# A routed two-layer network behind decayed attention: the weight narrowing's transfers move from SyncE's queue to ScalarE's

## The chip, the cores and the metric

The kernel runs on one core of a Trainium2 chip. A core has five engines that each work through their own list of instructions in order: TensorE (PE, matrix products; PEld is its loading of weights), VectorE (DVE), ScalarE (ACT), GpSimd (POOL) and SyncE (SP). They wait for each other through semaphores. SP computes nothing here; it reads a number and issues DMA transfers, which 16 DMA engines carry out. [...] The metric is the device time of one execution in microseconds (us), the median of three runs.

## What is computed

Three stages, in 32-bit floats. The 64-bit `w_in` and `w_out` at the end are the input's; the kernel gets them as raw 64-bit words (see below).

```python
# 1. causal attention without softmax, decayed by gamma_h ** (i - j): batch 4, 8 heads, 576 rows, 64 columns
scores = (q @ k.T) / sqrt(64)
x = (scores * Dmat) @ v                        # -> 2304 tokens of 512 features
# 2. each token goes to one of 8 experts, 288 tokens each, by descending logit x @ w_gate
order = np.argsort(-(x @ w_gate).flatten())    # first come, first served, until an expert is full
h = np.maximum(x[mask] @ w1[e], 0.0)           # 288 x 512 @ 512 x 1024
out[mask] = h @ w2[e]                          # 288 x 1024 @ 1024 x 512
# 3. a gated network over all tokens
h = x @ w_in                                   # 2304 x 512 @ 512 x 2048
out = (h * tanh(softplus(h))) @ w_out          # 2304 x 2048 @ 2048 x 512
```

## The kernel before

**Stages.** The attention fills the first 100 us. Behind it runs the expert stage: for each of eight experts, in the order in which they fill up, a search on VectorE and PE (the routing) finds the expert and its 288 tokens, GpSimd gathers the tokens' rows (`xg`), PE transposes them (`mmx`), and PE does 96 first products (`mma`, eight groups of 12) and 96 second products (`mmb`, four outputs of 24). Last come the products of the gated network, in six tiles of 384 tokens (`mmc` and `po`).

**Three products for one.** Products run in a reduced 32-bit format. Each operand is therefore split in a rounded part and a rest, and each product is done three times. For an expert's weights that is the work of `unit` and `split_unit`: SP loads a tile of 512 KB (`st`, five buffers), ScalarE rounds it (`whi`, L564), and GpSimd or VectorE subtracts (`wlo`, L567), which frees the `st` buffer. Eight such units make an expert. ScalarE and VectorE split the activations likewise: `xh` and `xl` of the gathered tokens, `hh` and `hl` of the first products' results. ScalarE also copies each second product from its bank to a buffer `y` (four of them, `YB`), which SP stores.

**The expert's number.** VectorE makes it (`eid`, L532). SP reads it (`value_load`, L534), for the address of the eight loads that follow.

**The list store.** SP stores the token numbers of an expert (`list_scratch`, L652): 288 numbers of 4 bytes, as 96 rows of 3.

**The narrowing.** [...] `narrow()` makes 32-bit copies of `w_in` and `w_out` from their 64-bit words, in 32 pieces beside the experts' work. For a piece SP loads 512 KB (`std`, three buffers); ScalarE scales the high words (`words`, one buffer in PSUM); VectorE shifts these and joins them with the low words' top bits (`words`, then `dw`, L730 and L733); ScalarE takes the sign (`dt`, L737); GpSimd multiplies (`dw`, L741); SP stores 256 KB (L744). The last stage's units are loaded from these copies.

**What sets the order.** A planner (`run_tasks`) writes every engine's list before the program runs. Each piece of work is a generator that yields an engine, an estimated duration, what must come before, and a priority; the planner takes, at estimated times, the first ready piece and appends its instructions to that engine's list. An estimate doesn't hold anything up on the chip, but the order that comes of it does: an instruction that waits there holds all that stands behind it on its engine.

Of the kernel before, what the change touches and what calls it, by code (L numbers as in the profile page):

```python
# [7 lines left out]
F32 = mybir.dt.float32  # L8
# [3 lines left out]
U32 = mybir.dt.uint32  # L12
# [5 lines left out]
P = 128  # L18
# [16 lines left out]
APART = 3000  # L35
NRING = 12
STAGES = 5
YB = 4
CLOSED = -1.0e37

PE, DVE, POOL, ACT, SP = "pe", "dve", "pool", "act", "sp"
HOP = 200
DMA_RATE = 350
DMA_ISSUE = 100
# [88 lines left out]
class Kernel:  # L133
# [389 lines left out]
    def weights_of(self, junk, at, i):  # L523

        nc, a, rw = self.nc, self.a, self.rw
        units = {}
        self.weights.append(units)
        n0 = len(self.weights) * 8 - 8
        at = yield DVE, 160, [at], EID
        eid = rw.tile([P, 1], I32, name="eid")  # L530
        with nc.allow_low_precision(reason="small integers"):
            nc.vector.tensor_reduce(eid, junk, AX.X, ALU.add)  # L532
        at = yield SP, 1000, [at if i == 0 else Event(at.t + APART)], 0
        e = nc.sync.value_load(eid[0:1, 0:1], min_val=0, max_val=E - 1)  # L534
        for u in range(8):
            if u < 4:
                src = a["w1"][bass.ds(e, 1), :, u * 256:(u + 1) * 256]
            else:
                src = a["w2"][bass.ds(e, 1), (u - 4) * 256:(u - 3) * 256, :]
            yield from self.unit(n0 + u, src.rearrange("o (k p) c -> p (o k) c", p=P),  # L540
                                 DVE if n0 == 0 and u < 2 else None, units, 3,
                                 *([lambda: self.fetched] if n0 == 0 and u == FIRST_UNITS else []))
# [122 lines left out]
    def y_place(self):  # L665

        n = self.made - YB
        return Event(0) if n < 0 else self.stored[n] if n < len(self.stored) else None
# [38 lines left out]
    def narrow(self):  # L707

        nc, v, ic, a = self.nc, self.nc.vector, self.ic, self.a
        done = {k: {} for k in ("load", "read", "turn", "shift", "sign", "store")}  # L710

        def at(k, n):
            return [lambda: done[k].get(n)] if n >= 0 else []

        def load():
            for n in range(32):
                name = ("w_in", "w_out")[n % 2]
                c, r = divmod(n // 2, a[name].shape[0] // P)
                r = slice(r * P, r * P + P)
                now = yield SP, DMA_ISSUE, [Event(0), *[lambda: self.apart(e()) for e in at("read", n - 3)]], self.narrow_priority  # L720
                st = self.conv.tile([P, 512, 2], U32, name="std", bufs=3)
                nc.sync.dma_start(st.rearrange("p c w -> p (c w)"), a[name].bitcast(U32)[r, c * 1024:c * 1024 + 1024])
                self.spawn(piece(n, st, self.arrival(524288, now), a[name + "32"][r, c * 512:c * 512 + 512]))

        def piece(n, st, now, dst):
            high, w = st[:, :, 1].bitcast(F32), self.words.bitcast(U32)
            now = yield ACT, 680, [now, *at("read", n - 1)], self.narrow_priority
            nc.scalar.activation(self.words, high, AF.Copy, scale=2.0 ** -112)
            now = yield DVE, 620, [now], self.narrow_priority
            v.tensor_scalar(w, w, ic[:, IC["three"]], None, op0=ALU.logical_shift_left)  # L730
            now = yield DVE, 680, [now, *at("store", n - 2)], self.narrow_priority
            out = self.conv.tile([P, 512], U32, name="dw", bufs=2)
            v.scalar_tensor_tensor(out, st[:, :, 0], ic[:, IC["low"]], w, op0=ALU.logical_shift_right, op1=ALU.bitwise_or)  # L733
            done["shift"][n] = now
            sign = yield ACT, 680, [*at("sign", n - 2), *at("shift", n)], self.narrow_priority
            t = self.conv.tile([P, 512], F32, name="dt", bufs=2)
            nc.scalar.sign(t, high)  # L737
            done["read"][n] = sign
            now = yield POOL, 1310, [now, sign], self.narrow_priority
            out = out.bitcast(F32)  # L740
            nc.gpsimd.tensor_tensor(out, out, t, op=ALU.mult)  # L741
            done["sign"][n] = now
            now = yield SP, DMA_ISSUE, [Event(now.t + APART)], self.narrow_priority
            nc.sync.dma_start(dst, out)  # L744
            done["store"][n] = self.arrival(262144, now)
            self.narrowed[n] = done["store"][n]

        self.spawn(load())

    def product(self, name, terms, first=True, last=True, bank=None):  # L750
# [20 lines left out]
    def experts(self):  # L771
        nc, a = self.nc, self.a
        for i in range(E):
# [14 lines left out]
            def result(i, d, bank, at):  # L788
                at = yield ACT, 410, [at, self.y_place], 0
                self.made += 1  # L790
                y = self.fa.tile([P, CAP], F32, name="y", bufs=YB)
                nc.scalar.copy(y, bank[1][:, :CAP])
# [292 lines left out]
```

## Time and profile before

| | us |
|---|---|
| runs (three) | 886.77, 889.37, 892.02 |
| median | 889.37 |
| the profiled execution's own time | 888.98 |
| its span, first to last instruction | 887.2 |
| PE busy | 805.0 (91%) |
| VectorE, ScalarE, GpSimd busy | 677.7, 408.2, 479.0 |

The profile is of one execution. In its rows a line such as L564 is a line of the kernel; `SPq` is SP issuing a transfer; `x96` counts instructions; a bracket `[7.29 <-ACT y L792]` says that the engine was idle for 7.29 us just before, and which instruction ended the wait. `out<-in` names tiles without their buffer numbers. PEclk is TensorE's granted clock as a share of full speed. A DMA share can read above 1, since it sums the time of packets.

### The profile page before, as it was taken

Reading aid. Unit: us, or ns where it says so; the run is one execution under the profiler, and the core shown is the slowest. Engines: PE = TensorE matmul, PEld = TensorE weight load, DVE = VectorE, ACT = ScalarE, POOL = GpSimd, SP = SyncE. Lnnn points to the kernel's source line nnn. Section 1 sums busy time; section 2 is a strip of 40 time slices with the busy share of each in tenths; the row PEclk is TensorE's granted clock in tenths of the full one; section 3 lists DMA queues with packets and bytes.
Section 4 is the critical chain, followed back from the end, with each engine's and each line's share of the span. In section 5 each row is a group of like instructions: output and inputs, shape, how many; then the busy total and the mean of one; then the engine's idle time right before and its main releaser. Section 6 shows DMA issues by size and latency. Waiting matters only on the chain. (4 is left out here: it accounts for less than half of the span.)

```text
span 887.2 us, 15492 instructions
## 1 busy us (share of the span) xinstructions
PE 805.0 (91%) x5834; PEld 722.4 (81%) x5837; DVE 677.7 (76%) x1102; ACT 408.2 (46%) x736; POOL 479.0 (54%) x408
## 2 busy tenths in 40 slices
PE   7999875959898987784989999999999999999997
PEld 5888734948798887784989998998999999999995
DVE  4444584846586766694776999999899899899894
ACT  1221223524353434454675654655655555555552
POOL 4533026473667656573511866756755755755644
PEclk9999768979798989796998999999999999999999
DMA  9982157786777876699894000100200100100000
GB/s 342 362 265 88 60 184 148 245 133 192 174 239 171 181 252 158 224 227 236 300 338 160 18 1 1 63 10 1 63 9 1 63 10 1 63 10 1 36 1 36
DMA packets 66331, 112.37 MB, mean 127 GB/s; under 512 B 10192, under 2 KB 38224, under 8 KB 66256
## 3 DMA queue, kind: packets, MB, share of 16 engines
q1 hardware_dynamic: 63280, 101.94, 39.8%
q0 software_dynamic: 2976, 9.44, 3.5%
q8 instruction: 46, 0.75, 0.4%
q14 instruction: 29, 0.24, 0.1%
HBM read 88.81 MB, written 22.55 MB: 126 GB/s over the span
## 5 line engine op out<-in xcount | busy, mean ns | idle before, releaser
L994 DVE RECIPROCAL q<-q 128x384 f32<-128x384 f32 x96 | 244.3, 2545 | 11.5 <-ACT q L992 7.2
L567 POOL TENSOR_TENSOR wlo<-st,whi 128x1024 fp32r<-128x1024 f32 x55 | 132.3, 2422 | 74.3 <-ACT whi L564 74.3
L996 POOL TENSOR_TENSOR n<-n,q 128x384 f32<-128x384 f32 x96 | 99.1, 1032 | 112.9 <-DVE q L994 101.8
L964 PE MATMUL mmc<-yl,whi 128*128 128x384 f32 x384 | 130.3, 339 | 5.8 <-DVE yl L924 3.4
L1006 POOL TENSOR_TENSOR gl<-n,gh 128x384 fp32r<-128x384 f32 x96 | 106.6, 1110 | 48.2 <-ACT gh L1004 47.8
L964 PE MATMUL mmc<-yh,whi 128*128 128x384 f32 x384 | 129.7, 338 | 0.7 <-ACT yh L921 0.7
L964 PE MATMUL mmc<-yh,wlo 128*128 128x384 f32 x384 | 130.0, 339 | 0.0
L564 ACT CAST whi<-st 128x1024 fp32r<-128x1024 f32 x80 | 82.6, 1045 | 90.8 <-DMA st<-w 85.3
L1025 PE MATMUL po<-whi,gl 128*128 128x512 f32 x288 | 113.9, 395 | 0.0
L1025 PE MATMUL po<-wlo,gh 128*128 128x512 f32 x288 | 113.7, 395 | 0.0
L1025 PE MATMUL po<-whi,gh 128*128 128x512 f32 x288 | 111.9, 389 | 0.0
L989 DVE SCALAR_TENSOR_TENSOR n<-s 128x384 f32<-128x384 f32 x96 | 103.9, 1084 | 2.6 <-ACT s L982 2.1
L982 ACT ACTIVATE s<-mmc 128x384 f32<-128x384 f32 x96 | 47.1, 491 | 126.3 <-PE mmc L964 121.1
L758 PE MATMUL mma<-xh,whi 128*128 128x288 f32 x256 | 81.4, 318 | 10.4 <-ACT xh L626 10.1
L758 PE MATMUL mmb<-hh,whi 128*128 128x288 f32 x256 | 82.4, 322 | 0.0
L964 PEld LDWEIGHTS mmc<-yl,whi 128*128 128x128 f32 x384 | 72.4, 189 | 11.8 <-DVE yl L924 4.4
L758 PE MATMUL mmb<-hl,whi 128*128 128x288 f32 x256 | 81.1, 317 | 0.0
L758 PE MATMUL mmb<-hh,wlo 128*128 128x288 f32 x256 | 80.9, 316 | 0.0
L758 PE MATMUL mma<-xh,wlo 128*128 128x288 f32 x256 | 80.1, 313 | 0.0
L758 PE MATMUL mma<-xl,whi 128*128 128x288 f32 x256 | 78.7, 307 | 0.1
L964 PEld LDWEIGHTS mmc<-yh,whi 128*128 128x128 f32 x384 | 72.4, 189 | 4.9 <-ACT yh L921 0.9
L741 POOL TENSOR_TENSOR dw<-dw,dt 128x512 f32<-128x512 f32 x32 | 43.0, 1346 | 61.4 <-ACT dt L737 24.9
(149 smaller groups left out, 1636.3 us busy)
## 6 DMA issues: line engine op xcount, KB each, us to landing
st<-w SPq DMA_DIRECT2D x64, 512.0 KB
qk<-qk SPq DMA_DIRECT2D x18, 512.0 KB
kv<-kv SPq DMA_DIRECT2D x18, 512.0 KB
std<-w_in SPq DMA_DIRECT2D x16, 512.0 KB
std<-w_out SPq DMA_DIRECT2D x16, 512.0 KB
x_scratch<-xs SPq DMA_DIRECT2D x18, 256.0 KB
y_scratch<-y SPq DMA_DIRECT2D x32, 144.0 KB
yt<-y_scratch SPq DMA_DIRECT2D x22, 192.0 KB
```

The lines of the kernel that those rows point to most:

```text
L564: self.nc.scalar.copy(dst[0], st)
L567: (self.nc.vector if lo.engine == DVE else self.nc.gpsimd).tensor_tensor(dst[1], st, dst[0].bitcast(F32), op=ALU.subtract)
L741: nc.gpsimd.tensor_tensor(out, out, t, op=ALU.mult)
L758: self.nc.tensor.matmul(bank[1][:, :CAP], al if h == 2 else ah, bl if h == 1 else bh, start=(first and j == h == 0), stop=(last and j == n ...
L964: self.nc.tensor.matmul(bank[1][:, :TILE], (wl if h == 2 else wh)[:, c, cs], x[c][h == 1], start=(c == h == 0), stop=(c == HP - 1 and h == 2))
L982: nc.scalar.activation(s, p, AF.Sigmoid)
L989: v.scalar_tensor_tensor(u, s, 2.0, s, op0=ALU.subtract, op1=ALU.mult)
L994: v.reciprocal(q, q)
L996: nc.gpsimd.tensor_tensor(u, u, q, op=ALU.mult)
L1006: nc.gpsimd.tensor_tensor(gl, u, gh.bitcast(F32), op=ALU.subtract)
L1025: nc.tensor.matmul(po[j], (gl if h == 2 else gh)[:, js], (wl if h == 1 else wh)[:, f % 2], start=(f == h == 0), stop=(f == DFF // P - 1 an ...
```

## The change

The narrowing's loads and stores are issued by ScalarE, in its own queue: right behind the sign of piece n it issues the store of piece n-2 and the load of piece n+3. The first three loads and the last two stores stay with SP. A third `dw` buffer is added, and one of the four `y` buffers is given up for it. In the planner, SP's read of an expert's number now follows the last load of the expert ahead; before, it followed the number by an estimated 3 us.

```diff
--- before.py
+++ after.py
@@ -35,7 +35,7 @@
 APART = 3000
 NRING = 12
 STAGES = 5
-YB = 4
+YB = 3
 CLOSED = -1.0e37
 
 PE, DVE, POOL, ACT, SP = "pe", "dve", "pool", "act", "sp"
@@ -530,7 +530,7 @@
         eid = rw.tile([P, 1], I32, name="eid")
         with nc.allow_low_precision(reason="small integers"):
             nc.vector.tensor_reduce(eid, junk, AX.X, ALU.add)
-        at = yield SP, 1000, [at if i == 0 else Event(at.t + APART)], 0
+        at = yield SP, 1000, [at, *([lambda: self.loaded.get(n0 - 1)] if n0 else [])], 0
         e = nc.sync.value_load(eid[0:1, 0:1], min_val=0, max_val=E - 1)
         for u in range(8):
             if u < 4:
@@ -712,38 +712,59 @@
         def at(k, n):
             return [lambda: done[k].get(n)] if n >= 0 else []
 
+        name = ("w_in", "w_out")
+        words, sent = {}, {}
+
+        def place(n):
+            c, r = divmod(n // 2, a[name[n % 2]].shape[0] // P)
+            return name[n % 2], slice(r * P, r * P + P), c
+
+        def fetch(n, queue):
+            if n < 32:
+                w, r, c = place(n)
+                words[n] = self.conv.tile([P, 512, 2], U32, name="std", bufs=3)
+                queue.dma_start(words[n].rearrange("p c w -> p (c w)"), a[w].bitcast(U32)[r, c * 1024:c * 1024 + 1024])
+
+        def send(n, queue):
+            if n >= 0:
+                w, r, c = place(n)
+                queue.dma_start(a[w + "32"][r, c * 512:c * 512 + 512], sent.pop(n))
+
         def load():
-            for n in range(32):
-                name = ("w_in", "w_out")[n % 2]
-                c, r = divmod(n // 2, a[name].shape[0] // P)
-                r = slice(r * P, r * P + P)
-                now = yield SP, DMA_ISSUE, [Event(0), *[lambda: self.apart(e()) for e in at("read", n - 3)]], self.narrow_priority
-                st = self.conv.tile([P, 512, 2], U32, name="std", bufs=3)
-                nc.sync.dma_start(st.rearrange("p c w -> p (c w)"), a[name].bitcast(U32)[r, c * 1024:c * 1024 + 1024])
-                self.spawn(piece(n, st, self.arrival(524288, now), a[name + "32"][r, c * 512:c * 512 + 512]))
-
-        def piece(n, st, now, dst):
-            high, w = st[:, :, 1].bitcast(F32), self.words.bitcast(U32)
-            now = yield ACT, 680, [now, *at("read", n - 1)], self.narrow_priority
+            now = yield SP, 3 * DMA_ISSUE, [Event(0)], self.narrow_priority
+            for n in range(3):
+                fetch(n, nc.sync)
+                self.spawn(piece(n, self.arrival(524288, now)))
+
+        def piece(n, now):
+            st, w = words[n], self.words.bitcast(U32)
+            high = st[:, :, 1].bitcast(F32)
+            now = yield ACT, 680, [now, *at("shift", n - 1)], self.narrow_priority
             nc.scalar.activation(self.words, high, AF.Copy, scale=2.0 ** -112)
             now = yield DVE, 620, [now], self.narrow_priority
             v.tensor_scalar(w, w, ic[:, IC["three"]], None, op0=ALU.logical_shift_left)
-            now = yield DVE, 680, [now, *at("store", n - 2)], self.narrow_priority
-            out = self.conv.tile([P, 512], U32, name="dw", bufs=2)
+            now = yield DVE, 680, [now, *at("store", n - 3)], self.narrow_priority
+            out = self.conv.tile([P, 512], U32, name="dw", bufs=3)
             v.scalar_tensor_tensor(out, st[:, :, 0], ic[:, IC["low"]], w, op0=ALU.logical_shift_right, op1=ALU.bitwise_or)
             done["shift"][n] = now
-            sign = yield ACT, 680, [*at("sign", n - 2), *at("shift", n)], self.narrow_priority
+            sign = yield ACT, 800, [now, *at("sign", n - 2), *at("turn", n - 1)], self.narrow_priority
             t = self.conv.tile([P, 512], F32, name="dt", bufs=2)
             nc.scalar.sign(t, high)
-            done["read"][n] = sign
+            done["turn"][n] = sign
+            send(n - 2, nc.scalar)
+            fetch(n + 3, nc.scalar)
+            if n >= 2:
+                self.narrowed[n - 2] = done["store"][n - 2] = self.arrival(262144, sign)
+            if n + 3 < 32:
+                self.spawn(piece(n + 3, self.arrival(524288, sign)))
             now = yield POOL, 1310, [now, sign], self.narrow_priority
-            out = out.bitcast(F32)
+            sent[n] = out = out.bitcast(F32)
             nc.gpsimd.tensor_tensor(out, out, t, op=ALU.mult)
             done["sign"][n] = now
-            now = yield SP, DMA_ISSUE, [Event(now.t + APART)], self.narrow_priority
-            nc.sync.dma_start(dst, out)
-            done["store"][n] = self.arrival(262144, now)
-            self.narrowed[n] = done["store"][n]
+            if n >= 30:
+                now = yield SP, DMA_ISSUE, [now], self.narrow_priority
+                send(n, nc.sync)
+                self.narrowed[n] = self.arrival(262144, now)
 
         self.spawn(load())
 
```

The change moves instructions in the lists of five engines. Three places are shown, all at the passage from expert 5 to expert 6 (experts count from 0). On SP the lines L550 are weight loads, L652 the list stores and the `y` stores, L534 the reads of a number, L722 and L744 (L726 and L731 after) the narrowing's loads and stores. First the kernel before, from the read of expert 7's number: the first list store below is expert 6's, the second expert 7's; the three loads ahead of the second one are expert 6's sixth to eighth.

```order
L534 TENSOR_LOAD eid_5202
L534 ISA x2
L550 ISA
L550 DMA st_5332<-w2 128x2x512
L652 DMA list_scratch<-idx_5206 96x3x1
L550 ISA
L550 DMA st_5357<-w2 128x2x512
L722 DMA std_5384<-w_in 128x1024
L550 ISA
L550 DMA st_5393<-w2 128x2x512
L652 DMA list_scratch<-idx_5317 96x3x1
L744 DMA w_out32<-dw_5336 128x512
```

In the changed kernel, from expert 6's eighth load, which follows expert 6's list store, to the first `y` store of expert 5:

```order
L550 ISA
L550 DMA st_5338<-w2 128x2x512
L534 TENSOR_LOAD eid_5181
L534 ISA x2
L550 ISA
L550 DMA st_5386<-w1 128x4x256
L652 DMA list_scratch<-idx_5304 96x3x1
L550 ISA
L550 DMA st_5418<-w1 128x4x256
L550 ISA
L550 DMA st_5435<-w1 128x4x256
L652 DMA y_scratch<-y_5412 128x288
```

The narrowing's transfers are gone from here, the read of expert 7's number has moved behind expert 6's eighth load, and expert 7's first load stands ahead of expert 7's list store.

On ScalarE, before: the rounding of expert 6's sixth to eighth tile (`whi`) and the four roundings of its tokens (`xh` of `mmx6`).

```order
L792 COPY y_5407<-mmb51_5312 128x288
L564 CAST whi_5415<-st_5332 128x1024
L626 CAST xh_5216<-mmx6_5420 128x288
L626 CAST xh_5216<-mmx6_5424 128x288
L626 CAST xh_5216<-mmx6_5430 128x288
L564 CAST whi_5450<-st_5357 128x1024
L564 CAST whi_5466<-st_5393 128x1024
L792 COPY y_5479<-mmb52_5403 128x288
L737 ACTIVATE dt_5487<-std_5116 128x512
L626 CAST xh_5216<-mmx6_5490 128x288
```

After, the same tokens' roundings, with expert 6's seventh and eighth tile around them:

```order
L752 ACTIVATE dt_5371<-std_4864 128x512
L731 DMA w_in32<-dw_4983 128x512
L726 DMA std_5374<-w_out 128x1024
L743 ACTIVATE words_1379<-std_4993 128x512
L564 CAST whi_5395<-st_5310 128x1024
L813 COPY y_5412<-mmb50_5329 128x288
L626 CAST xh_5212<-mmx6_5408 128x288
L626 CAST xh_5212<-mmx6_5414 128x288
L626 CAST xh_5212<-mmx6_5421 128x288
L626 CAST xh_5212<-mmx6_5425 128x288
L813 COPY y_5444<-mmb51_5330 128x288
L564 CAST whi_5455<-st_5338 128x1024
```

The four `xh` now stand together ahead of the eighth tile's `whi`, and a store and a load of the narrowing (L731, L726) stand behind each `dt`.

On VectorE, before: the last parts of the tokens' split (`xl`) of expert 6 around the narrowing's `dw` number 23, counted from 0.

```order
L567 TENSOR_TENSOR wlo_5295<-st_5156,whi_5294 128x1024
L628 TENSOR_TENSOR xl_5217<-mmx6_5420,xh_5216 128x288
L628 TENSOR_TENSOR xl_5217<-mmx6_5424,xh_5216 128x288
L628 TENSOR_TENSOR xl_5217<-mmx6_5430,xh_5216 128x288
L733 SCALAR_TENSOR_TENSOR dw_5472<-std_5116,ic_567,words_1379 128x512
L567 TENSOR_TENSOR wlo_5451<-st_5357,whi_5450 128x1024
L628 TENSOR_TENSOR xl_5217<-mmx6_5490,xh_5216 128x288
L730 TENSOR_SCALAR words_1379<-words_1379,ic_567 128x512
```

After:

```order
L745 TENSOR_SCALAR words_1379<-words_1379,ic_567 128x512
L567 TENSOR_TENSOR wlo_5257<-st_5106,whi_5256 128x1024
L628 TENSOR_TENSOR xl_5213<-mmx6_5408,xh_5212 128x288
L628 TENSOR_TENSOR xl_5213<-mmx6_5414,xh_5212 128x288
L628 TENSOR_TENSOR xl_5213<-mmx6_5421,xh_5212 128x288
L628 TENSOR_TENSOR xl_5213<-mmx6_5425,xh_5212 128x288
L748 SCALAR_TENSOR_TENSOR dw_5459<-std_4993,ic_567,words_1379 128x512
L567 TENSOR_TENSOR wlo_5456<-st_5338,whi_5455 128x1024
```

All four `xl` stand ahead of that `dw` now.

## Rows read from the trace of the kernel before

**Rows 1.** The page, part 1: busy us (share of the span) and instructions.

```profile
PE 805.0 (91%) x5834; PEld 722.4 (81%) x5837; DVE 677.7 (76%) x1102; ACT 408.2 (46%) x736; POOL 479.0 (54%) x408
```

**Rows 2.** The chain that ended last: start us, us, what.

```profile
607.05 2.10 PE mmc L964 x12
```

**Rows 3.** Stretches: us, busy PE, PEld, DVE, ACT, POOL, PEclk, DMA share, GB/s.

```profile
120.00:480.00 360.00, 300.13 (x2536) 272.55 (x2537) 242.46 (x658) 163.51 (x276) 194.79 (x111) 0.88 0.79 214
480.00:880.00 400.00, 397.52 (x1991) 359.26 (x1991) 378.69 (x288) 221.20 (x421) 245.01 (x244) 1.00 0.07 23
...
211.00:215.00 4.00, 4.00 (x43) 3.87 (x42) 3.68 (x8) 3.27 (x5) 2.07 (x1) 1.00 0.95 336
389.00:396.00 7.00, 7.00 (x58) 7.00 (x57) 7.00 (x2) 3.39 (x7) 6.98 (x5) 1.00 1.08 80
401.00:409.00 8.00, 2.31 (x18) 1.94 (x17) 0.00 (x0) 0.00 (x0) 0.00 (x0) 0.76 1.30 103
```

**Rows 4.** Stretches, `mma` alone: busy PE, PEld, DVE, ACT, PEclk, DMA, GB/s.

```profile
415.00:430.00 15.00, 14.69 (x96) 14.18 (x96) 2.93 (x7) 2.86 (x7) 0.87 1.05 368
442.70:455.50 12.80, 12.80 (x96) 12.60 (x96) 2.79 (x7) 2.85 (x7) 1.00 1.00 333
```

**Rows 5.** PE's waits from 120 to 470 us: total, times, longest.

```profile
PE pD L457 <- DVE sat L373: 18.2, 7, 7.0
PE mmx L636 <- ACT y L792: 10.2, 3, 7.3
```

**Rows 6.** Timeline of PE, 393 to 417 us: start, us, what, idle before.

```profile
400.10 0.47 PE L636 MATMUL mmx<-cst,xg 96*128 96x96 f32 x3 [3.33 <-DVE xl L628]
...
410.86 0.74 PE L636 MATMUL mmx<-cst,xg 96*128 96x96 f32 x3 [7.29 <-ACT y L792]
414.59 0.74 PE L636 MATMUL mmx<-cst,xg 96*128 96x96 f32 x3 [2.99 <-DVE xl L628]
```

**Rows 7.** Timeline of ScalarE, pieces from 340 to 416 us.

```profile
357.73 1.04 ACT L564 CAST whi<-st 128x1024 fp32r<-128x1024 f32 x1 [7.50 <-DMA st<-w]
...
387.84 0.65 ACT L737 ACTIVATE dt<-std 128x512 f32<-128x512 f32 x1
...
409.46 1.04 ACT L564 CAST whi<-st 128x1024 fp32r<-128x1024 f32 x1 [9.18 <-DMA st<-w]
```

**Rows 8.** Timeline of VectorE, pieces from 348 to 418 us.

```profile
358.51 0.75 DVE L733 SCALAR_TENSOR_TENSOR dw<-std,ic,words 128x512 uint32<-128x512 uint32 x1 [7.69 <-DMA w_in<-dw]
...
412.28 0.75 DVE L733 SCALAR_TENSOR_TENSOR dw<-std,ic,words 128x512 uint32<-128x512 uint32 x1 [11.51 <-DMA w_out<-dw]
```

**Rows 9.** Timeline of SP's issues, 365 to 430 us.

```profile
386.07 0.41 SPq L652 DMA_DIRECT2D list_scratch<-idx  x1
...
397.91 0.38 SPq L550 DMA_DIRECT2D st<-w  x1
398.34 0.45 SPq L652 DMA_DIRECT2D list_scratch<-idx  x1
398.90 0.46 SPq L744 DMA_DIRECT2D w_out<-dw  x1
```

**Rows 10.** Tile `eid`: ns min/median/max, first and last start us.

```profile
L532 DVE TENSOR_REDUCE eid<-junk x8: 134/154/156, 120.2 to 379.2; 128x1 int32<-128x8 f32 x8
L534 SPq TENSOR_LOAD <-eid x8: 267/274/463, 120.4 to 379.4; - x8
```

**Rows 11.** SP's waits over the whole span: total us, times, longest.

```profile
SPq L550 <- POOL wlo L567: 59.8, 16, 6.2
SPq L722 <- DVE dw L733: 43.9, 13, 16.8
```

**Rows 12.** Tile `std`, SP's issues: ns min/median/max, first and last start.

```profile
L722 SPq DMA_DIRECT2D std<-w_in x16: 328/375/1463, 134.8 to 434.3; - x16
```

**Rows 13.** Tile `dw`, who waited for it (its store): total us, times.

```profile
  DVE dw L733: 32.2, 8
```

## The prediction, made before the changed kernel was run

> **What bounds the kernel now.** I read the page first, then the chain of waits, the busy time in stretches, the waits of TensorE, and the timeline around its longest stops. The page [rows 1] shows TensorE (PE) busy for 805.0 of 887.2 us. The chain that ended last [rows 2] stands, from about 605 us, on groups of the first and second product in turn, the first at 2.10 us. The stretch from 480 to 880 us [rows 3] has PE busy for 397.52 of 400 us at full granted clock, so what the change does there can be worth no more than 2.5 us. The time to be won lies ahead of it, in the expert stage from 120 to 480 us, where PE is busy for only 300.13 of 360 us and the granted clock is 0.88 on average [rows 3].
>
> What stops PE there? TensorE's waits [rows 5] name VectorE's `sat` (18.2 us) and ScalarE's `y` (10.2 us): two engines that work in order and had something else to finish first. The largest stops are at the passage from expert 5 to expert 6 [rows 6]: idle for 3.33 us until 400.10, for 7.29 us until 410.86 and for 2.99 us until 414.59, 13.6 us in all. ScalarE [rows 7] stood for 9.18 us until 409.46 in the rounding of a weight tile that had not landed; the `y` copy and the fourth `xh` were behind it. VectorE [rows 8] stood for 11.51 us until 412.28 in the narrowing's `dw`, for the store of an earlier `dw`; an `xl` was behind it.
>
> Both waited for transfers in the same stretch. SyncE (SP) issued the eighth load of expert 6 at 397.91, expert 7's list store at 398.34, and that `dw` store at 398.90 [rows 9]. From 401 to 409 us the DMA engines moved 103 GB/s although their share reads as fully busy; after expert 6's list store at 386.07 they moved 80 GB/s from 389 to 396 us; in the free stretch from 211 to 215 us it was 336 GB/s [rows 3, 9]. The pattern stands behind each of the eight list stores (two are shown): some 3 us after the issue a slow stretch of 7 to 8 us. What PE loses in it depends on which engine then stands in a wait for a landing. The change doesn't take the list stores away; it moves what is in flight around them.
>
> **The change part by part.**
>
> The expert's number. VectorE makes it eight times, first at 120.2 and last at 379.2 us, and SP reads it from 120.4 to 379.4 [rows 10]. It was read as soon as it was made, so another place for the read is worth 0 for experts 1 to 6. For expert 7 the read now stands behind expert 6's eighth load instead of ahead of its sixth. Its own loads had to wait for that eighth load at 397.91 anyway [rows 9], and expert 7's products begin only at 442.7 [rows 4], so this costs 0 too. If that cover were gone it would cost the 18.5 us from 379.4 to 397.91 at most.
>
> SP's queue. 59 of its 64 narrowing transfers (29 loads, 30 stores) go to ScalarE; three loads and two stores stay. SP's 43.9 us of waiting for `dw` go [rows 11]. That is no gain by itself: the expert loads in the same queue waited 59.8 us for a stage buffer, which GpSimd's `wlo` frees [rows 11]. Five loads of an expert leave at once and the others one per `wlo`. I take 0 for experts 1 to 5, and look at expert 6, where the order around the list stores decides.
>
> The passage from expert 5 to 6. Term A: in ScalarE's new order all four `xh` of expert 6 stand ahead of the rounding of its eighth tile, so the 7.29 us go that PE waited behind that rounding. Term B: `dw` number 23 now needs store 20 instead of store 21, and ScalarE issues store 20 right behind `dt` number 22, which ran at 387.84 for 0.65 us [rows 7]. That is 10 us ahead of the 398.90 at which the store left that VectorE waited for; it may lie in the first slow stretch, but has landed at its end. All four `xl` stand ahead of that `dw`, too. PE's 2.99 us go. Late next is the gather of expert 7, for which the 3.33 us stay. Term C: from 401 to 409 us PE had 2.31 us of work, and expert 6's 96 first products then took 15.0 us at clock 0.87, against 12.8 us for expert 7's at 1.00 [rows 3, 4]. With 10.3 of the 13.6 us of idling gone I take half of these 2.2 us, 1.1 us.
>
> ScalarE's new work. 59 issues at some 0.35 us (SP's took 0.328 at least and 0.375 in the median [rows 12]) are 20.6 us. ScalarE is busy for 163.5 of 360 us in this stage [rows 3], so most of this lies in idle time. The cover fails where an `hh`, `xh` or `y` that PE needs stands right behind a pair. I take one pair of 0.7 us on the path in each of experts 1 to 5, 3.5 us (term D), between 0 and 20.6 us. The waits that come with the issues are hardly new: `dt` already waits for the product two pieces back, which reads the buffer that it writes, and the rounding of the next piece into `words` already waits for the `dw` that the load needs. Behind them on ScalarE stand `hh` and `y`, and PE's banks wait for these.
>
> Experts 1 to 5 otherwise. In experts 3 to 5 all eight loads now stand ahead of the list store on SP, so a wait such as ScalarE's 7.50 us until 357.73 [rows 7] should go there. Against it, GpSimd now has one or two more `wlo` ahead of each gather, so that the gather instead of the load is in flight in the slow stretch; and store n-3 now leaves only behind `dt` n-1. I take 0 for the sum. The ends are -18.2 us (all that PE waited for `sat`) and +16.5 us (rival 2 below).
>
> The fourth `y` buffer. A copy now waits for the store three back. That matters in one place: the last `y` of expert 5 needs the store of the first, which is queued behind expert 7's list store and two loads. PE goes on with four other banks meanwhile, at 1.6 us each (12.8 us for eight [rows 4]), so 0 is taken, between 0 and A + B = 10.3 us.
>
> The sum: 888.98 (the profiled execution's own time, that is the span of 887.2 and 1.8 around it) - 7.29 - 2.99 - 1.1 + 3.5 = 881.1 us. The median of the runs shown, 889.37, is 0.4 us above the profiled one, so I predict 881.5 us.
>
> A rule that speaks against it. In one queue an expert's first five loads have none of the narrowing between them, and the DMA engines then moved 336 GB/s from 211 to 215 us [rows 3]. The Trainium skill (DMA: Bandwidth & Descriptors, Queues, rings and completion order) says that each DMA engine takes turns between the queue rows that have work, and that SP and ScalarE own one row each. By the row the first loads lose nothing; by the rule a narrowing load and store go beside them and take their share. What that would make of the time is rival 3.
>
> **The rivals.** (1) No change: the last `y` of expert 5 stands on ScalarE until the first one's store has landed, behind expert 7's list store. For it: the `dw` store that left behind a list store at 398.90 freed its reader only at 412.28 [rows 8, 9]. Against it: PE has banks for 6.4 us more. It gives back A and B: 881.5 + 10.3 = 892 us at most, and 890 if the banks cover a little. (2) Slower, by late stores: in the middle experts store n-3 leaves so late that the slow stretch catches it, VectorE stands in `dw` n, and `sat` and PE with it, as at 358.51, where VectorE stood for 7.69 us and PE's longest wait for `sat` was 7.0 us [rows 5, 8]. VectorE's eight waits for stores sum to 32.2 us [rows 13]; without the 7.69 and the 11.51 the other six average 2.2 us. If one wait rises from 2.2 to 7.69 in each of experts 2 to 4, that is 3 x 5.5 = 16.5 us: 898 us. It decides wherever the store leaves less than some 3 us ahead of the slow stretch. (3) Slower, by shared bandwidth: one narrowing load and store, 768 KB at 336 GB/s, put 2.3 us into the head of each of seven experts' loads: 16.4 us if all of it reaches PE, 898 us. Against it: PE is still busy with the expert ahead when these loads land (4.00 of 4.00 us from 211 to 215 [rows 3]). (4) Faster still: the 7.0 us of `sat` in expert 5 go too, since its loads pass its list store: 874.5 us.
>
> **How the numbers follow.** I call a difference under 0.5% (4.4 us) no change. The forecast has 0.40, with its own range 876 to 887; rival 4 has 0.15, rival 1 0.22, rival 2 0.16, rival 3 0.07. Faster is the forecast less its upper edge (0.06), with rival 4: 0.49. Same is that edge and rival 1, less 0.01: 0.27. Slower is rivals 2 and 3 and this 0.01: 0.24. The range 867 to 899 holds rival 4 with 7 us to spare, and both slow rivals at its high end: the order of five engines moves at once, and the unknown costs (D up to 20.6, experts 1 to 5 from -18.2 to +16.5) are wide.
>
> **What would show it.** Right: PE's idle time between the last product of expert 5 and the first of expert 6 falls from 13.6 to 3 to 5 us, the `xh` of expert 6 come without a wait for a weight tile, the slow stretches behind the list stores are still there, and the time from expert 6's first product to the end keeps its length. Wrong: ScalarE stands for over 5 us in a `y` behind a store (rival 1); VectorE's waits for stores grow beyond 32.2 us and PE's for `sat` beyond 18.2 (rival 2); the first loads of an expert land later after its number is made (rival 3); or the idle time moves to the gathers, which the forecast puts at 3.33 us.

## The result: 1.2% slower, and the profile after

The changed kernel took 898.5 us in the median of 14 runs, the kernel before 886.8 us beside it: a ratio of the means of 1.0122 (95% interval 1.0093 to 1.0151); the medians give 1.0132. The forecast was 881.5 us. Ratios, here and below, leave out executions that took over 1.5% longer than the fastest of their kernel; for e9 below that is six of twelve, and with them its ratio is 0.993 instead of 0.989. The profiled execution took 901.2 us, its span 899.4 us against 887.2. Its page lists ScalarE's transfers under a queue of their own (q10, 23.07 MB).

The stretches of the page show where to look. The columns are those of [rows 3].

```profile
120.00:480.00 360.00, 295.15 (x2479) 266.42 (x2477) 230.31 (x656) 159.45 (x266) 197.48 (x110) 0.88 0.81 210
480.00:880.00 400.00, 395.53 (x1996) 358.85 (x1997) 379.29 (x289) 223.22 (x423) 239.48 (x238) 1.00 0.08 26
```

In the expert stage PE is busy for 5.0 us less than before in the same 360 us, at the same clock [rows 3]: it waits more. PE's waits of that stretch (total, times, longest):

```profile
PE pD L457 <- DVE sat L373: 31.5, 7, 9.3
PE pF L452 <- DVE known L439: 10.3, 5, 7.9
PE mmx L636 <- ACT y L813: 8.3, 1, 8.3
```

`sat` and `known` are made by VectorE; the first stood at 18.2 us before [rows 5]. VectorE's own waits of the same stretch say what it had been doing:

```profile
DVE dw L748 <- DMA w_in<-dw: 35.5, 7, 9.6
DVE dw L748 <- DMA w_out<-dw: 25.4, 5, 10.3
```

That is 60.9 us in twelve waits, against 32.2 in eight [rows 13]. In each, VectorE stands in the narrowing's `dw` number n because the store of number n-3 has not landed. Of VectorE's timeline (start us, us, engine line, operation, in brackets the idle time before it and what ended it) the four that made PE stop for longest, numbers 3, 6, 11 and 19:

```profile
190.04 0.75 DVE L748 SCALAR_TENSOR_TENSOR dw<-std,ic,words 128x512 uint32<-128x512 uint32 x1 [9.64 <-DMA w_in<-dw]
...
228.67 0.75 DVE L748 SCALAR_TENSOR_TENSOR dw<-std,ic,words 128x512 uint32<-128x512 uint32 x1 [8.23 <-DMA w_out<-dw]
...
280.02 0.75 DVE L748 SCALAR_TENSOR_TENSOR dw<-std,ic,words 128x512 uint32<-128x512 uint32 x1 [9.05 <-DMA w_in<-dw]
280.69 0.15 DVE L373 TENSOR_SCALAR sat<-pF 31x8 bf16<-31x8 f32 x1
...
360.46 0.75 DVE L748 SCALAR_TENSOR_TENSOR dw<-std,ic,words 128x512 uint32<-128x512 uint32 x1 [6.67 <-DMA w_in<-dw]
```

The third of them, in expert 3, with the `sat` behind it, read through the other engines. SP's issues, the list store:

```profile
261.92 0.47 SPq L652 DMA_DIRECT2D list_scratch<-idx  x1
```

ScalarE, store 8, and a weight tile that was on its way as well:

```profile
266.25 0.33 ACTq L731 DMA_DIRECT2D w_in<-dw  x1
...
277.95 1.04 ACT L564 CAST whi<-st 128x1024 fp32r<-128x1024 f32 x1 [9.41 <-DMA st<-w]
```

And PE:

```profile
280.88 0.16 PE L457 MATMUL pD<-sat,digit 31*128 31x8 bf16 x1 [8.36 <-DVE sat L373]
```

The stretch between, ahead of it and in it:

```profile
262.00:268.00 6.00, 6.00 (x50) 5.50 (x48) 4.38 (x11) 3.43 (x7) 4.41 (x5) 0.85 1.14 368
268.00:278.00 10.00, 4.53 (x58) 3.96 (x58) 2.17 (x7) 0.59 (x3) 5.22 (x3) 0.80 1.12 60
```

The store left 4.3 us behind the list store and less than 2 us ahead of ten microseconds in which the DMA engines moved 60 GB/s; it landed when these were over. The four `dw` held PE for 9.27, 7.88, 8.36 and 5.97 us. The stores that they waited for, numbers 0, 3, 8 and 16, left 0.9, 0.7, 4.3 and 3.2 us behind the list stores of experts 1, 2, 3 and 5. In the kernel before one stop of over 5 us had this form, the 7.0 us of [rows 5] behind the 7.69 of [rows 8].

The passage to expert 6 lost its old waits and got a new one. ScalarE has no wait for the eighth weight tile left there. It stands in a load of the narrowing, which must wait for `dw` 22, which waits for store 19:

```profile
394.73 0.66 ACT L752 ACTIVATE dt<-std 128x512 f32<-128x512 f32 x1
406.70 0.33 ACTq L726 DMA_DIRECT2D std<-w_out  x1
407.08 0.64 ACT L743 ACTIVATE words<-std 128x512 f32<-128x512 f32 x1 [11.70 <-DVE dw L748]
407.65 1.04 ACT L564 CAST whi<-st 128x1024 fp32r<-128x1024 f32 x1
408.58 0.39 ACT L813 COPY y<-mmb 128x288 f32<-128x288 f32 x1
```

The `y` for which PE waited is the last of these rows; PE went on at 409.03:

```profile
409.03 0.74 PE L636 MATMUL mmx<-cst,xg 96*128 96x96 f32 x3 [8.31 <-ACT y L813]
```

The stretches of the first products of experts 6 and 7, `mma` alone, answer to [rows 4], which began at 415.00 and 442.70:

```profile
419.80:436.10 16.30, 13.66 (x96) 12.74 (x96) 1.81 (x4) 2.06 (x5) 1.00 0.89 309
449.60:463.00 13.40, 13.12 (x96) 12.65 (x96) 1.71 (x4) 2.74 (x7) 1.00 0.86 290
```

### The profile page after: what moved, and what is told of

The parts are those of the page before. It is cut to its first block, busy times and chain, and to the rows that moved or that the text cites. A ratio compares the mean times of both kernels' runs of the same rounds, so it can differ in the third digit from the quotient of the medians.

```text
span 899.4 us, 15469 instructions
## 1 busy us (share of the span) xinstructions
PE 812.2 (90%) x5837; PEld 727.3 (81%) x5837; DVE 671.7 (75%) x1102; ACT 410.2 (46%) x736; POOL 482.2 (54%) x408
## 3 DMA queue, kind: packets, MB, share of 16 engines
q1 hardware_dynamic: 54784, 78.87, 28.3%
q10 hardware_dynamic: 8496, 23.07, 12.2%
## 4 chain that ended last, share of the span: by engine, by line
PE 53%; DMA 19%; DVE 14%; issue 5%; POOL 4%; ACT 3%; SPq 1%; POOLq 0%; ACTq 0%; DVEq 0%
PE mmc L985 16%; PE po L1046 15%; DMA st<-w 6%; DVE q L1015 5%; DMA w_in<-dw 5%; PE mmb L779 5%; PE mma L779 4%; DMA w_out<-dw 4%; DVE n L1010 3%; PE pA L202 2%; PE pT L233 2%; PE pL L243 2%; DMA y_scratch<-y 2%; PE pT L230 2%; DMA std<-w_in 2%
## 5 line engine op out<-in xcount | busy, mean ns | idle before, releaser
L762 POOL TENSOR_TENSOR dw<-dw,dt 128x512 f32<-128x512 f32 x32 | 46.7, 1460 | 85.8 <-ACT dt L752 35.1
```

## Experiments

Theory S: stores that leave two tiles late, through ScalarE, fall into the slow stretches behind the list stores, and VectorE stands behind them. The rivals put the loss on the loads' queue or on the number's new rule. The ratios below are to the kernel before on the same chip, where its median was 872.5 to 877.3 us; in brackets is the 95% interval. The changed kernel ran only beside the 886.8 us of the result, so it is compared with these runs by its ratio, and expectations in us are to be read as ratios too. "Store waits" are VectorE's waits in `dw` for stores in the profiled execution; between the changed kernel and these runs they compare only roughly.

**e1 and e2: half of the queue move each.** e1 issues the stores from SP, right behind their product; the loads stay with ScalarE.

```diff
-            send(n - 2, nc.scalar)
...
-            if n >= 30:
-                now = yield SP, DMA_ISSUE, [now], self.narrow_priority
-                send(n, nc.sync)
+            now = yield SP, DMA_ISSUE, [Event(now.t + APART)], self.narrow_priority
+            send(n, nc.sync)
```

> The changed kernel with one part undone: every store of a narrowed piece leaves from SyncE again, right behind its product, and only the loads stay on ScalarE. Theory S (the store of piece n-3 leaves a piece too late, the slow stretch behind a list store catches it, and VectorE stands in dw n): back to the kernel before, 883 to 891 us, and VectorE's waits for these stores fall from 60.9 us to 35 us or less. Rival Q (the loads in a second queue take bandwidth from the experts' loads) and rival E (the other place of the number's read reorders all engines): still 895 to 902 us.

Measured: 0.9998 (0.9967 to 1.0028); store waits 11.8 us in four:

```profile
DVE dw L748 <- DMA w_out<-dw: 9.3, 2, 8.1
DVE dw L748 <- DMA w_in<-dw: 2.5, 2, 1.5
```

e2 issues the loads from SP and leaves the late stores on ScalarE.

```diff
+        def refill(n, now):
+            now = yield SP, DMA_ISSUE, [Event(now.t + APART)], self.narrow_priority
+            fetch(n, nc.sync)
+            self.spawn(piece(n, self.arrival(524288, now)))
...
-            fetch(n + 3, nc.scalar)
...
-                self.spawn(piece(n + 3, self.arrival(524288, sign)))
+                self.spawn(refill(n + 3, sign))
```

> The other half: the loads leave from SyncE again, the stores stay on ScalarE behind the sign two pieces on. Theory S: still slow, 894 to 902 us, VectorE's waits for stores over 50 us. Rival Q: back to 883 to 891 us. Rival E: 895 to 902 us as well.

Measured: 1.0216 (1.0162 to 1.0269); store waits 35.3 us, where theory S had over 50. The loss stays with the stores. That e2 is worse than the whole change, with fewer store waits, I cannot explain.

**e3 and e4: no list stores beside the experts.** Both keep the eight lists in a constant's tile and store them in the last stage; e3 is the kernel before with this, e4 the changed one.

```diff
-        idx = rw.tile([GB, 3], I32, name="idx", bufs=3)
+        idx = self.kept[i]
...
-        self.spawn(self.store(a["list"][i * CAP:(i + 1) * CAP].rearrange("(g b) -> b g", b=GB), idx, at))
...
+        yield SP, 3000, [lambda: self.loaded.get(E * 8 + 15), at], 2.6
+        for i in range(self.listed_to, ((t + 1) * W - 1) // CAP + 1):
+            nc.sync.dma_start(a["list"][i * CAP:(i + 1) * CAP].rearrange("(g b) -> b g", b=GB), self.kept[i])
```

> The kernel before, with the eight list stores taken out of the expert stage: each is issued in the last stage, just before the tile that needs it (the token numbers stay in 96 bytes of a constants' tile until then). Theory S says that the slow stretches come from these stores: they go, PE's idle time from 120 to 470 us falls from some 60 to 25 us or less, 845 to 865 us. If the slow stretches have another cause, the stretches stay and the time is 882 to 892 us.

> The changed kernel with the list stores moved to the last stage in the same way. Theory S: without slow stretches the late stores are caught by nothing, so it comes to within 5 us of the kernel before with late list stores. Rivals Q, E and Y (three y buffers instead of four): it stays 8 to 14 us above that one.

Measured: e3 0.9667 (0.9631 to 0.9703), e4 0.9762 (0.9725 to 0.9799). The list stores cost the kernel before 3.3%; PE's busy time of the expert stage rises from 300.1 us [rows 3] to this in e3:

```profile
120.00:480.00 360.00, 336.63 (x2774) 306.89 (x2773) 282.60 (x694) 190.31 (x327) 222.02 (x133) 0.95 0.68 218
```

The slow stretches are gone. Cut in pieces of 3 us from 120 to 430 us, the kernel before has ten pieces with a DMA share above 0.8 and less than 150 GB/s; e3 has none, and e4, e8, e10 and e12 below have none either. The gathers are still there, so they are not the source: expert 3's leaves from 236.7 us on in e3, and behind it the trace shows

```profile
240.00:250.00 10.00, 9.63 (x110) 8.46 (x109) 6.64 (x22) 4.15 (x7) 9.98 (x7) 1.00 0.76 257
```

But e4 stays some 1% above e3, so the slow stretches are not the whole of the loss. The next runs look for the rest.

**e5: each store one tile earlier.** Still from ScalarE, behind sign n instead of n+1's.

```diff
-            send(n - 2, nc.scalar)
+            send(n - 1, nc.scalar)
```

> The changed kernel, with store n-1 instead of n-2 issued by ScalarE behind sign n, so each store leaves one tile (about 10 us) earlier and only the last store stays on SP. Theory S (stores leave too late, VectorE stands in dw behind them): about half of the loss comes back, ratio to the kernel before 1.000 to 1.008, VectorE's waits in dw for stores 35 to 45 us instead of 60.9. Rival Y (the loss is the three y buffers, not the stores): 1.012 as the changed kernel, and ScalarE's waits in y for stores stay at about 10 us. New risk: the issue on ScalarE now stands behind GpSimd's product of the tile before; if that costs, ScalarE shows waits in dt and the ratio stays at 1.012.

Measured: 1.0023 (0.9991 to 1.0056), as theory S has it for the ratio; store waits only 3.8 us, far under its 35 to 45.

**e6: the old rule for the number.**

```diff
-        at = yield SP, 1000, [at, *([lambda: self.loaded.get(n0 - 1)] if n0 else [])], 0
+        at = yield SP, 1000, [at if i == 0 else Event(at.t + APART)], 0
```

> The changed kernel with the expert's number read by the old rule (a fixed 3 us behind its making) instead of behind the loads of the expert ahead. Theory S: the rule is worth nothing, ratio to the kernel before 1.009 to 1.016, waits in dw for stores 55 to 65 us. Rival E (the rule holds up expert 7's list, gather and loads, and these meet the narrowing's transfers): ratio 1.006 or less, expert 7's first product at least 4 us nearer to expert 6's.

Measured: 1.0022 (0.9989 to 1.0056), store waits 13.6 us. Theory S alone is wrong here: the late stores are all there, and 1.0% comes back. The rule matters, though expert 7's first product is only 1.5 us nearer to expert 6's (28.3 us instead of 29.8), not 4. What the rule moves is GpSimd's order. Its timeline around expert 3's gather, in the changed kernel (number made at 248.0 us):

```profile
254.40 7.08 POOL L567 TENSOR_TENSOR wlo<-st,whi 128x1024 fp32r<-128x1024 f32 x3 [8.61 <-ACT whi L564]
261.62 0.94 POOL L614 DMA_INDIRECT xg<-x_scratch,idx  x1
```

and in e6 (number made at 231.0):

```profile
239.17 2.40 POOL L567 TENSOR_TENSOR wlo<-st,whi 128x1024 fp32r<-128x1024 f32 x1 [5.87 <-ACT whi L564]
241.72 0.94 POOL L614 DMA_INDIRECT xg<-x_scratch,idx  x1
```

The gather, with the list store 0.3 us behind it in experts 2 to 5, leaves 13.6 us behind the number instead of 10.7, and 11.4, 10.6, 13.2 and 13.0 instead of 8.3, 10.2, 10.1 and 10.5 in experts 1, 2, 4 and 5. In e6 store 7 leaves ScalarE just ahead of SP's list store of expert 3:

```profile
242.00 0.34 ACTq L731 DMA_DIRECT2D w_out<-dw  x1
```

```profile
242.08 0.41 SPq L652 DMA_DIRECT2D list_scratch<-idx  x1
```

The `dw` that needs it, number 10, ran at 249.57 us without a wait. From here on theory M is that the loss is the meeting of the two.

**e7 and e9: the buffers alone, and with the rule.** e7 is the kernel before with three `dw` and three `y`; e9 adds the new rule (the edit of e6 the other way round).

```diff
-YB = 4
+YB = 3
...
-            now = yield DVE, 680, [now, *at("store", n - 2)], self.narrow_priority
-            out = self.conv.tile([P, 512], U32, name="dw", bufs=2)
+            now = yield DVE, 680, [now, *at("store", n - 3)], self.narrow_priority
+            out = self.conv.tile([P, 512], U32, name="dw", bufs=3)
```

> The kernel before with the changed kernel's buffers alone: three y buffers instead of four, three dw buffers instead of two, so dw n waits for store n-3; queues and order rule as before. Theory S: the stores leave early here, so the third dw can only help: VectorE's waits in dw fall from 32.2 to 10 us or less, ratio 0.985 to 1.000. Rival Y (the fourth y buffer carries the loss): ratio 1.005 or more, ScalarE's y copies wait for stores by 8 us or more.

> The kernel of e7 (the kernel before with three dw and three y buffers, all transfers still issued by SP) with the new rule for the expert's number. Theory M (a meeting: the new rule puts the list store later behind the loads, and only together with stores that leave two tiles late does a store fall into the slow stretch just ahead of its reader): the rule alone costs little, ratio 0.984 to 0.994, waits in dw for stores 15 us or less. Rival R (the rule has a price of its own of 1%, as e6 against the changed kernel could be read): ratio 0.996 or more.

Measured: e7 0.9876 (0.983 to 0.9922), store waits 7.8 us; e9 0.989 (0.9843 to 0.9936), store waits 10.7 us. The buffers together are a gain of 1.2% that the change contains. What the missing `y` costs by itself was not measured; ScalarE's `y` copies wait for stores by 7.4 us in e7, just under rival Y's 8. The rule by itself is free, or nearly so, while SP issues everything. Yet in e9 too the gathers of experts 1 to 5 leave later, 11.9 to 13.4 us behind the number against 9.8 to 10.9 in e7, so a later gather is not a loss in itself.

**e13 and e14: which half of the rule, and the price of the loads.** e13 reads behind the loads of the expert ahead, as the change does, but lets the planner allow the 3 us of the old rule; e14 is e1 with the old rule.

```diff
-        at = yield SP, 1000, [at, *([lambda: self.loaded.get(n0 - 1)] if n0 else [])], 0
+        at = yield SP, 1000, [at if i == 0 else Event(at.t + APART), *([lambda: self.loaded.get(n0 - 1)] if n0 else [])], 0
```

> The changed kernel with both halves of the old and the new rule: the number is read behind the loads of the expert ahead, and the planner again allows 3 us between its making and its read. Against e6 (old rule) only the read of expert 7's number moves on SP, by three loads; the order on GpSimd is that of e6. Theory G (what costs is the dropped 3 us: it puts loads, one or two more wlo and so the gather and the list store in another order): ratio to the kernel before 0.999 to 1.006, as e6, waits in dw for stores 25 us or less. Rival H (what costs is that expert 7's number is held up): 1.009 to 1.015, as the changed kernel.

> The kernel of e1 (loads issued by ScalarE, stores by SP right behind the product) with the old rule. It completes the set with e1, e6 and e7. If the loads on ScalarE have a price by themselves (e1 stands 1.1% above e9, which has the same buffers and rule and its loads on SP): 0.996 to 1.003, as e1. If e1's price came from the new rule's order: 0.984 to 0.992, as e7.

Measured: e13 1.0025 (0.9995 to 1.0055), with store waits of 31.2 us, more than expected; e14 0.9876 (0.9821 to 0.993), store waits 18.3 us. So the later read for expert 7 costs nothing that shows; the 1% comes with the 3 us less, which reorder `wlo`, gather and list store. And the loads on ScalarE are free under the old rule: e14 equals e7. But e1 differs from e14 in the rule alone and is 1.2% above it, with its stores as early. The price of the rule needs no late stores, which theory M takes as its condition; it shows wherever ScalarE issues the loads beside list stores.

**e11: the list store alone moved.** The changed kernel, with the list store planned 6 us later, behind the eighth load.

```diff
-        self.spawn(self.store(a["list"][i * CAP:(i + 1) * CAP].rearrange("(g b) -> b g", b=GB), idx, at))
+        self.spawn(self.store(a["list"][i * CAP:(i + 1) * CAP].rearrange("(g b) -> b g", b=GB), idx, Event(at.t + 2 * APART)))
```

> The changed kernel with one edit: the list store is planned 6 us later, so that it stands behind the expert's eighth load and one or two more stores of y on SP. Queues, buffers and the rule stay. Theory M: where the list store stands against store n-3 decides, so the time moves by over 0.5% although nothing is taken away; a store now has some 3 us more to land, so VectorE's waits in dw for stores fall from 60.9 to 45 us or less and the ratio to the kernel before to 1.007 or less. Rival L (late stores cost by themselves, wherever the list store is): 1.009 to 1.016, waits 55 us or more. If the waits rise instead, the meeting is with another store than the one I take.

Measured: 1.0051 (1.002 to 1.0082), store waits 15.5 us. Nothing was taken away, and more than half of the loss is gone: where the list store stands decides much of it. The fall of the store waits fits a meeting of list store and narrowing store, as theory M has it, but does not show that this is the only way.

**e8, e10 and e12: without list stores beside the experts.** e8 is e1, e10 is e6 and e12 is e7, each with the edit of e3.

> The changed kernel with its stores issued by SP right behind the product (as in e1), and the list stores moved to the last stage (as in e3 and e4). If the late stores are also what keeps e4 1% above e3: ratio 0.964 to 0.970, as e3's 0.967. If what keeps e4 above is something else of the change (order rule, y buffers, ScalarE's issues): 0.973 to 0.980, as e4's 0.976.

> The kernel of e4 (changed kernel, list stores in the last stage) with the old rule for the expert's number. Without list stores beside the experts there is no slow stretch for a store to meet. Theory M: the rule is worth under 0.3% here, ratio 0.973 to 0.980 as e4, whose rest over e3 comes from the late stores alone (e8 without them was at 0.9665). Rival R: ratio 0.970 or less.

> The kernel of e7 (three dw and three y buffers, queues and rule as before) with the list stores moved to the last stage as in e3. If the third dw only helps against the slow stretches, there is nothing left for it: ratio 0.963 to 0.970, as e3. If it helps by itself (the two gains add): 0.955 to 0.960.

Measured: e8 0.9665 (0.9622 to 0.9707), e10 0.9656 (0.9611 to 0.9702), e12 0.9638 (0.9589 to 0.9686). With the list stores gone, neither the queue of the stores nor the third `dw` makes a difference to e3's 0.9667 that shows. e10 went against my theory M: only the new rule beside late stores (e4) stays above. e12 has the lowest ratio, with an interval that overlaps those of e3, e8 and e10; it beats both kernels, the one before by 3.6%.

## Why the prediction was wrong

One way through the ratios gives the change as a sum of steps: the buffers -1.2% (e7), the loads on ScalarE 0 (e14), the stores on ScalarE behind the sign of n+2 +1.5% (e6 against e14), the rule's order +1.0% (the changed kernel against e6). Together that is +1.2%, each step good to 0.4 to 0.7%.

Other ways through give other steps. The late stores cost in each of the three pairs that differ in them: +1.5%, +1.2% (the changed kernel against e1) and, roughly alike otherwise, +3.3% (e2 against e9); issued one tile earlier they are back at e1's ratio (e5). So they are shown as a cause. The rule costs +1.0% with late stores, +1.2% with early ones (e1 against e14) and nothing that shows with the loads on SP (e9 against e7). The loads on ScalarE cost 0 under the old rule, +1.1% under the new one (e1 against e9) and -0.9% beside late stores (the changed kernel against e2). Each edit also gives the planner another order for all engines, and such a change of order by itself may be behind a step of 1%; no run separates that.

- **What bounds it** held: the time is decided ahead of 480 us, in waits of engines that work in order, and the slow stretches behind the list stores are its main source: without them PE idles for 23.4 of the 360 us instead of 59.9 (e3).
- **The step that failed is "Experts 1 to 5 otherwise. ... I take 0 for the sum."** The same paragraph names what changed: "GpSimd now has one or two more `wlo` ahead of each gather" and "store n-3 now leaves only behind `dt` n-1". I set them against a wait for a weight tile that would go, and called it even. A later gather is not a loss in itself (e9), but the late stores alone measure 1.2 and 1.5% in the two pairs that differ in nothing else. Rival 2's mechanism is what happened: VectorE's store waits 60.9 us instead of 32.2, PE's for `sat` 31.5 instead of 18.2. It had 0.16. That its 898 us is nearly the measured 898.5 is luck: it adds three longer waits, in experts 2 to 4, to a forecast whose gains at the passage did not come, and the four longest are in experts 1, 2, 3 and 5. It named no cause for the stores being caught there and not before; e6, e11 and e13 point to the place of gather and list store, e1 and e9 say that this is not all of it.
- **Where it went.** The profiled execution took 20.1 us more than the 881.1 forecast for it: 1.2 ahead of expert 5's first product (4.7 us lost, where term D had 3.5), 11.5 at the passage, 7.4 behind it. So the smallest part of the miss stands in the stretch of the zero itself, where the longer waits meet what the buffers give back; the largest stands in the passage, where a late store was taken for landed.
- **Terms A, B and C** (-11.4 us together) came to nothing. From expert 5's first `mma`, at 369.2 us before and 373.9 after, to expert 6's it is 45.8 and 45.9 us. A's mechanism was right: the wait for the eighth tile is gone. B's was not: I took store 20 for landed, but VectorE stood in `dw` 22, one earlier, for store 19, issued at 392.3, 1.6 us behind the list store of 390.7. PE's 8.31 us for `y` replace the 7.29; term C's clock came (1.00 instead of 0.87), but the first products of expert 6 took 16.3 us with new waits in them. That resembles rival 1, but the `y` was held by a load's issue on ScalarE, not by its own buffer. The prediction had called "the waits that come with the issues" hardly new; new is that their `dw` waits longer.
- **Term D** was sized about right for one issue, 0.33 us instead of 0.35, and too high on the path: 29 of them, the loads, cost nothing that shows under the old rule (e14).
- **The fourth `y` buffer** at 0 is not refuted by e7, which gains with three; but ScalarE's waits in `y` for stores, none before, are 7.4 us in two there and 10.2 in two in the changed kernel. Its price alone stays open.
- **The expert's number** at 0 held for the read (e13) and failed for the planner: the 3 us that the rule no longer allows changed GpSimd's order, which costs 1.0 to 1.2% with the loads on ScalarE.
- **"The time from expert 6's first product to the end keeps its length"** failed: 479.6 us of the span behind 419.8, against 472.2 behind 415.0. Of these 7.4 us, 2.1 lie between expert 6's first product and expert 7's and 4.7 between that (449.6 against 442.7) and the last stage's (474.2 against 462.6). There VectorE stood for 5.33 us until 459.96 in the last `dw` for store 28, and PE for 2.86 us until 474.24 for ScalarE's `yh`; that one led to the other is not shown.
- **Rival 3**, shared bandwidth at the head of each expert, is not shown: e14 has the narrowing's loads in a second queue beside the expert's first loads and loses nothing to e7. The 1.1% of e1 above e9 leaves room for it under the new rule, but the changed kernel lies below e2, which has its loads on SP.

Open: by which way the new rule costs 1% where ScalarE issues the loads, with early stores as with late ones, and beside late stores even where no list store is near (e4 against e10); and why e2 is above the whole change. Store waits of one profiled execution order the kernels only roughly: e13 with 31.2 us and e6 with 13.6 have the same ratio, and e1's trace is of an execution 9 us below its median.

## What to carry to other kernels

A store that frees a buffer belongs right behind the work that fills it; put behind a later instruction of a busy engine it needs that much more time to spare, and here two tiles were not enough. A planner's allowance, here 3 us between making and reading a number, is part of the order of every engine: before calling an edit of it free, compare what stands ahead of each gather and each wait, and price that by the row, not by setting a gain against a loss of unknown size. Change buffers and queues apart, since a gain of one (-1.2%) hides in the loss of the other (+2.5%). And measure an edit beside more than one state of the others: here moving the loads cost 1.1% or nothing, or gained 0.9%, as the rule and the stores stood.

## What the runs showed of the hardware

Eight list stores of 1.1 KB each, in 4-byte pieces, cost the kernel before 3.3% (e3), and 2.4 to 3.7% in the four other pairs with and without them (e4, e8, e10 and e12, each against its kernel with list stores). The slow stretch behind one reads as fully busy DMA engines that move 60 GB/s for 10 us, where 368 GB/s were moved in the 6 us ahead. It holds up what either queue has in flight: here a weight load of SP and a store of ScalarE. An issue on ScalarE takes 0.33 us of its sequencer in the median (at most 1.04 in the changed kernel, 3.6 in e1); 29 of them cost no time that shows in e14.
